# Gated linear attention with a max-out layer behind it: the first three units and the loop's steps put in another order, with dummy matmuls in the gaps

## The chip, the core and the metric

The kernel runs on one core of a Trainium2 chip. A core has five engines with a queue of their own each: TensorE (PE in the profile; its weight loads are PEld), VectorE (DVE), ScalarE (ACT), GpSimd (POOL) and SyncE (SP), which here only issues loads. The metric is the device time of one execution in microseconds (us). It is compared as the median of several executions.

## The reference

Inputs are q, k, v and alpha of shape 4 x 8 x 768 x 48 (batch, head, time, head dimension) and three weight matrices. For every batch and head a 48 x 48 state is carried through time; then all heads of one time step are joined to one row of 384 values, and a two-branch layer is applied.

```python
for t in range(S):
    state = alpha[:, :, t, :, None] * state + np.einsum('bhd,bhe->bhde', k[:, :, t], v[:, :, t])
    y[:, :, t] = np.einsum('bhd,bhde->bhe', q[:, :, t], state)
...
x = np.ascontiguousarray(attn_out.transpose(0, 2, 1, 3)).reshape(B * S, H * D)
g = np.maximum(x @ w1, x @ w2)
return (g @ w_out).astype(np.float32)
```

There are 3072 rows of x, 384 columns, and 1024 hidden columns. The output is 3072 x 384 in float32.

## The kernel before, in words

**Units.** Time is cut into 6 chunks of 128 steps and the batch into 2 groups of 2, which makes 12 units; unit u holds chunk u // 2 of group u % 2. `bb` (0 or 1) is the batch inside a unit. The state passes from unit u to unit u + 2, so units 0 and 1 have no state ahead of them.

**Steps of one unit.** `load` (L85) puts the DMAs of alpha, k, q and v on SP's queue: two for alpha, one each for k, q, v (in units 0 and 1 one for each batch). `ln` (L157) takes the logarithm of alpha on ACT. `sums` (L171) forms running sums of it by matmul (tile `cs`, L181) and per-half totals (L184), and ACT takes exponentials: `Em` (L193), `cs` in place (L195) and `de` (L197). `kmul` (L214, POOL) and `qmul` (L218, DVE) scale k and q; `vcast` (L164, POOL) turns v into 16 bit; `state` (L199, POOL) scales the carried state. `turn` (L222) transposes scaled k and q on PE into one PSUM tile `tp`, which DVE copies to `qk`. `kv` (L232) is K^T V on PE, added into `tm` by DVE. `pairs` (L255) gives the 128 x 128 products `pp` on PE, which DVE multiplies by a triangular mask into `pt` (L265). `ystate` (L267) and `yin` (L281) add up y in PSUM, ACT copies it to `xn`; `xturn` (L296) transposes it on PE and DVE copies it to `xt`. In units 0 and 1 `yfirst` and `xfirst` (L306, L319) do the last three for one batch at a time. `hid` (L341) makes a quarter of the hidden layer: 6 matmuls and a ReLU into `gT`, on ACT for quarters 0 to 2 and on DVE for quarter 3. `hidhalf` (L327) does half the hidden layer for one batch. `outp` (L359) makes 128 rows of output: 3 matmuls of `xt` by `w2o` and 8 of `gT` by `wo16`, a copy on ACT, and with n = 1 the output's DMA, issued from ACT's queue.

**Weights.** max(a, b) is taken as ReLU(a - b) + b. So the hidden layer uses w12 = w1 - w2 (`wsub`, L402, DVE, a quarter at a time), and b W_out is x (w2 w_out): `wturn` (L378) casts a third of w2 on ACT, transposes it on PE and copies it on DVE; `wmul` (L387) multiplies it by w_out in two halves of 12 matmuls, and ACT copies the product to `w2o`. `dummies` (L408) issues matmuls of 512 columns on a zero tile; nothing reads them.

**What sets the order.** The order is written out by hand (L422 to L511), and every engine works its own queue in just that order. PSUM comes from four rings: "g" with 4 buffers (cs, tp, kv, ya, xp), "pp" with 2 (pp), "m" with 2 (hp, op, wt, dummies). A step that takes a buffer waits until its last reader is done. Loads have 4 buffers for each input.

## Time and profile before

| what | value |
|---|---|
| median of 13 runs | 165.71 us (165.07 to 166.66) |
| profiled execution | 165.52 us, its span 163.8 us |
| mean granted PE clock | 0.937 |
| PE busy | 143.8 us, 88% of the span |
| DVE, ACT, POOL busy | 92.6, 79.9, 47.1 us |
| read from and written to memory | 23.59 and 4.72 MB |

The span runs from the first to the last instruction; 1.7 us lie around it. The profile's page cuts the span into 40 slices with a digit for the busy tenths of each engine; the row PEclk gives the clock that PE was granted in tenths. A row of a timeline gives start and length in us, engine, line, operation, tile written and tiles read, how many such instructions follow each other, and in brackets the idle time before it and what ended that. A row of the view by windows gives the stretch, its length, then busy time with the number of instructions for PE, PEld, DVE, ACT and POOL, the granted clock, the share of the 16 DMA engines and GB/s.

### The profile page before, as it was taken

The numbers are of one execution on the slowest core, as the hardware profiler recorded it, in microseconds if no ns is written. First come the engines' busy times: TensorE is split into PE (matmuls) and PEld (weight loads), VectorE is DVE, ScalarE is ACT, GpSimd is POOL, SyncE is SP. The second block draws the span as 40 slices with busy tenths as digits, with TensorE's granted clock in tenths as the row PEclk, the third lists the DMA queues.
The fourth block names the chain that finished last, engine by engine and source line by source line (L and its number), as shares of the span: only waits on it lengthen the run. The fifth ranks groups of instructions, "written<-read, shape, count | busy, mean of one in ns | idle before, by whom it ended". The sixth has DMA issues, their size and how long they took to land.

```text
span 163.8 us, 4099 instructions
## 1 busy us (share of the span) xinstructions
PE 143.8 (88%) x1673; PEld 99.7 (61%) x1673; DVE 92.6 (57%) x191; ACT 79.9 (49%) x166; POOL 47.1 (29%) x73
## 2 busy tenths in 40 slices
PE   6845689994598969999999999999999999999892
PEld 2234435743476557676776776867767677676660
DVE  5064765107604986839569486595774955746110
ACT  3445041861058266737466375563764646643431
POOL 5023220033006280811706208054090350800000
PEclk9996556999569999999999999999999999999999
DMA  4999999999899997995993997989999962020202
GB/s 93 217 365 247 366 313 148 194 189 240 159 200 190 168 240 135 167 195 136 195 205 91 211 257 128 212 183 210 241 186 230 181 92 98 4 96 0 100 0 96
DMA packets 93459, 28.58 MB, mean 174 GB/s; under 512 B 87424, under 2 KB 93056, under 8 KB 93440
## 3 DMA queue, kind: packets, MB, share of 16 engines
q1 hardware_dynamic: 90160, 23.60, 79.4%
q10 hardware_dynamic: 3280, 4.72, 8.7%
q8 instruction: 13, 0.21, 0.6%
q14 instruction: 6, 0.05, 0.1%
HBM read 23.59 MB, written 4.72 MB: 173 GB/s over the span
## 4 chain that ended last, share of the span: by engine, by line
PE 74%; DVE 12%; ACT 5%; DMA 2%; issue 2%; POOL 1%; SPq 0%; ACTq 0%; DVEq 0%
PE op L368 19%; PE hp L350 18%; PE op L366 8%; PE pp L263 4%; PE tp L227 4%; PE wq L395 4%; DVE xt L304 3%; DVE pt L265 3%; PE cs L181 3%; DMA af<-in_alpha_dram 2%; PE ya L287 2%; DVE qk L229 2%; PE xp L302 2%; PE cs L184 2%; PE kv L243 2%
## 5 line engine op out<-in xcount | busy, mean ns | idle before, releaser
L216 POOL TENSOR_TENSOR kn<-kf,Em 128x384 f16<-128x384 f32 x24 | 23.5, 998 | 90.0 <-PE pp L263 48.3
L368 PE MATMUL op<-wo,gT 128*128 128x384 f16 x192 | 35.1, 326 | 0.0
L350 PE MATMUL hp<-xt,w 128*128 128x256 f16 x264 | 32.5, 273 | 2.7 <-DVE xt L304 2.7
L265 DVE TENSOR_TENSOR pt<-pp,u 128x512 f16<-128x512 f32 x48 | 30.9, 684 | 4.0 <-PE pp L263 3.6
L350 PEld LDWEIGHTS <-w 128*128 128x128 f16 x264 | 25.0, 97 | 7.9 <-issue 4.3
L355 ACT ACTIVATE gT<-hp 128x512 f16<-128x512 f32 x33 | 19.7, 597 | 16.7 <-PE hp L350 15.3
L368 PEld LDWEIGHTS <-gT 128*128 128x128 f16 x192 | 18.8, 98 | 12.4
L371 ACT COPY outs<-op 128x384 f32<-128x384 f32 x24 | 11.5, 478 | 28.8 <-PE op L368 28.7
L229 DVE COPY qk<-tp 128x1024 f16<-128x1024 f16 x24 | 16.4, 687 | 6.6 <-PE tp L227 6.5
L220 DVE TENSOR_TENSOR qn<-qf,cs 128x384 f16<-128x384 f32 x24 | 12.3, 549 | 10.8 <-ACT de L197 7.0
L251 DVE TENSOR_TENSOR tm<-kv,sb 64x192 f32<-64x192 f32 x32 | 11.3, 355 | 9.2 <-PE kv L243 8.4
L366 PE MATMUL op<-w2o,xt 128*128 128x384 f16 x72 | 15.8, 329 | 0.3 <-DVE gT L357 0.2
L193 ACT ACTIVATE Em<-cs 128x384 f32<-128x384 f32 x24 | 11.7, 487 | 8.6 <-PE cs L184 8.6
L304 DVE COPY xt<-xp 128x768 f16<-128x768 f16 x10 | 5.6, 557 | 14.5 <-PE xp L302 14.5
L263 PE MATMUL pp<-qk 48*128 48x128 f16 x192 | 11.2, 224 | 2.3 <-DVE qk L229 2.2
L357 DVE TENSOR_SCALAR gT<-hp 128x512 f16<-128x512 f32 x11 | 7.5, 685 | 7.9 <-PE hp L350 7.6
L195 ACT ACTIVATE cs<-cs 128x384 f32<-128x384 f32 x24 | 11.7, 489 | 0.0
L160 ACT ACTIVATE lg<-af 128x768 f16<-128x768 f32 x12 | 10.1, 840 | 3.4 <-DMA af<-in_alpha_dram 3.4
L227 PE MATMUL tp<-ident,qn 128*128 128x128 f16 x96 | 9.8, 227 | 1.7 <-DVE qn L220 1.6
L169 POOL CAST v<-vf 128x768 f16<-128x768 f32 (+1 forms) x14 | 10.2, 732 | 0.8 <-DMA vf<-in_v_dram 0.8
L227 PE MATMUL tp<-ident,kn 128*128 128x128 f16 x96 | 9.5, 222 | 0.8 <-POOL kn L216 0.8
L263 PEld LDWEIGHTS <-qk 48*128 48x128 f16 x192 | 6.2, 96 | 4.9 <-DVE qk L229 2.9
(60 smaller groups left out, 158.6 us busy)
## 6 DMA issues: line engine op xcount, KB each, us to landing
af<-in_alpha_dram SPq DMA_DIRECT2D x24, 192.0 KB, 5.5
out_dram<-outs ACTq DMA_DIRECT2D x11, 384.0 KB, 4.6
kf<-in_k_dram SPq DMA_DIRECT2D x10, 384.0 KB, 6.2
qf<-in_q_dram SPq DMA_DIRECT2D x10, 384.0 KB, 4.6
vf<-in_v_dram SPq DMA_DIRECT2D x10, 384.0 KB, 6.3
w2f<-in_moe_w_dram SPq DMA_DIRECT2D x3, 512.0 KB, 5.1
wof<-in_moe_w_out_dram SPq DMA_DIRECT2D x2, 768.0 KB, 6.9
w1f<-in_moe_w_dram SPq DMA_DIRECT2D x4, 384.0 KB, 8.7
```

Of the source, the lines that this page charges most:

```text
L193: nc.scalar.activation(out=Em, in_=csv[bb], func=ACTF.Exp, scale=-1.0)
L195: nc.scalar.activation(out=csv[bb], in_=csv[bb], func=ACTF.Exp)
L216: nc.gpsimd.tensor_mul(out=X["kn"][bb][:, :, 0:D], in0=X["kf"][:, bb], in1=X["Em"][bb])
L220: nc.vector.tensor_mul(out=X["qn"][bb][:, :, 0:D], in0=X["qf"][:, bb], in1=X["csv"][bb])
L227: nc.tensor.transpose(tp[:, n, j, :], pair(src, j), ident)
L229: nc.vector.tensor_copy(out=qk, in_=tp)
L263: nc.tensor.matmul(pa[a][:, j, :], lhsT=qk[r, 1, j, :], rhs=qk[r, 0, j, :], start=True, stop=True)
L265: nc.vector.tensor_mul(out=pt[:, a], in0=pa[a], in1=u16.unsqueeze(1).to_broadcast([128, HP, C]))
L350: nc.tensor.matmul(hp[:, n, :], lhsT=w12[:, ds, f * 128 : (f + 1) * 128], rhs=X["xt"][:, ds].rearrange("p n t -> p (n t)"), start=(ds == 0 ...
L355: nc.scalar.activation(out=gT[:, 2 * f2 : 2 * f2 + 2, :], in_=hp, func=ACTF.Relu)
L366: nc.tensor.matmul(op, lhsT=X["xt"][:, ds, n, :], rhs=w2o[:, ds, :], start=(ds == 0), stop=False)
L368: nc.tensor.matmul(op, lhsT=X["gT"][:, f, n * C : (n + 1) * C], rhs=wo16[:, f, :], start=False, stop=(f == NF - 1))
```

## The change

Nothing is computed in another way, except that `hidhalf` is gone and unit 1 uses `hid`, like all other units. The rest is order. `sums` is cut so that the exponentials are steps of their own (`expm`, `expp`, `expd`; `exps` is all of them), and the small sums come first. `first` gives way to `scale` (kmul, qmul, vcast), `turn`, `kv` and `pairs` written one by one. The casts of w2 leave `wturn`, those of w_out leave `wmul` (`wcast`), and so do the copies to `w2o` (`wout`). Unit 1's alpha is loaded ahead of w1. In units 0 and 2 there are 39 dummy matmuls in place of 17.

```diff
+    load_alpha(1)
     for n in range(4):
...
         nc.sync.dma_start(out=w1f[:, :, f], in_=moe_w1.rearrange("(s p) f -> p s f", p=128)[:, :, f])
-    load_alpha(1)
...
     dummies(10)
     ln(0)
     sums(0)
-    dummies(4)
-    first(0, 0)
+    exps(0)
+    dummies(6)
+    scale(0, 0)
+    for ds in range(ND):
+        nc.scalar.copy(out=w2h[:, ds, :], in_=w2f[:, ds, :])
+    turn(0, 0)
+    kv(0, (0,))
+    dummies(2)
+    pairs(0, 0)
+    dummies(2)
     wturn(0)
     yfirst(0, 0)
+    dummies(2)
     wturn(1)
+    dummies(2)
     xfirst(0, 0)
     wturn(2)
-    first(0, 1)
+    scale(0, 1)
+    dummies(2)
+    turn(0, 1)
+    kv(0, (1,))
+    dummies(3)
+    pairs(0, 1)
     load(2)
-    dummies(3)
+    dummies(6)
+    wcast(0)
     yfirst(0, 1)
+    wmul(0)
     xfirst(0, 1)
-    wmul(0)
+    wcast(1)
     wmul(1)
-    for n in range(4):
-        wsub(n)
-        hid(0, n)
-
     ln(1)
-    outp(0, 0)
+    wout()
+
     sums(1)
     load(3)
+    wsub(0)
+    wsub(1)
+    hid(0, 0)
+    expm(1, 0)
+    hid(0, 1)
+    expp(1, 0)
+    wsub(2)
+    wsub(3)
+    hid(0, 2)
+    expm(1, 1)
+    expp(1, 1)
+    scale(1, 0)
+    hid(0, 3)
+    expd(1)
+    turn(1, 0)
+    kv(1, (0,))
+    outp(0, 0)
+    scale(1, 1)
+    pairs(1, 0)
+    load(4)
+    turn(1, 1)
+    kv(1, (1,))
+    yfirst(1, 0)
     outp(0, 1)
-    first(1, 0)
-    load(4)
-    yfirst(1, 0)
-    first(1, 1)
+    pairs(1, 1)
+    ln(2)
     xfirst(1, 0)
-    hidhalf(1, 0, 0)
-    hidhalf(1, 0, 1)
+    sums(2)
+    dummies(2)
     yfirst(1, 1)
-    ln(2)
-    outp(1, 0)
-    sums(2)
+    exps(2)
+    dummies(2)
     xfirst(1, 1)
-    hidhalf(1, 1, 0)
-    hidhalf(1, 1, 1)
     for bb in range(2):
         kmul(2, bb)
+    state(2)
+    vcast(2)
+    for bb in range(2):
         qmul(2, bb)
-    vcast(2)
-    state(2)
+    hid(1, 0)
+    hid(1, 1)
+    turn(2, 0)
+    hid(1, 2)
+    turn(2, 1)
+    hid(1, 3)
     load(5)
-    turn(2, 0)
-    turn(2, 1)
...
     for u in range(2, NU):
+        pairs(u, 0)
+        kv(u)
         if nxt:
             ln(u + 1)
-        kv(u)
-        pairs(u, 0)
         if u > 2:
-            hid(u - 1, 2)
-            hid(u - 1, 3)
+            hid(u - 1, 0)
+            hid(u - 1, 1)
         else:
-            outp(1, 1)
+            outp(1, 0)
         if nxt:
             sums(u + 1)
+            exps(u + 1)
...
-        ystate(u)
         pairs(u, 1)
         if u > 2:
-            outp(u - 1, 0)
+            hid(u - 1, 2)
+        ystate(u)
+        if u > 2:
+            hid(u - 1, 3)
...
         yin(u)
+        outp(u - 1, 0 if u > 2 else 1)
         if nxt:
             turn(u + 1, 0)
-        if u > 2:
-            outp(u - 1, 1)
         xturn(u)
         if nxt:
             turn(u + 1, 1)
-        hid(u, 0)
-        hid(u, 1)
+        if u > 2:
+            outp(u - 1, 1)
...
-    hid(NU - 1, 2)
-    hid(NU - 1, 3)
+    for f2 in range(4):
+        hid(NU - 1, f2)
```

Three places in the queues follow; line numbers before and after differ, the tiles' names do not.

ACT in unit 0, before: from the first cast of w2 (w2h) to unit 1's logarithm (lg).

```order
L379 CAST w2h<-w2f 128x1024
L317 CAST xn<-yb 128x384
L379 CAST w2h<-w2f 128x1024 x2
L317 CAST xn<-yb 128x384
L391 CAST wo_168<-wof 128x768 x2
L400 CAST w2o<-wq 128x384 x3
L355 ACTIVATE gT<-hp 128x512 x3
L160 ACTIVATE lg_128<-af 128x16x48
```

ACT in unit 0, now:

```order
L431 CAST w2h<-w2f 128x1024 x3
L333 CAST xn<-yb 128x384
L404 CAST wo_168<-wof 128x768
L333 CAST xn<-yb 128x384
L404 CAST wo_168<-wof 128x768
L160 ACTIVATE lg_128<-af 128x16x48
L401 CAST w2o<-wq 128x384 x3
L357 ACTIVATE gT<-hp 128x512
L197 ACTIVATE Em<-cs 128x384
```

All casts of w2 now stand ahead of the first copy of y (xn), unit 1's logarithm stands ahead of the copies to w2o, and its exponentials stand between unit 0's ReLUs (gT).

ACT in one iteration of the loop, before: ReLUs of two units (gT), the next unit's logarithm and exponentials, the copies of the output (outs) and of y (xn).

```order
L355 ACTIVATE gT<-hp 128x512 x2
L160 ACTIVATE lg_130<-af 128x16x48
L355 ACTIVATE gT<-hp 128x512
L193 ACTIVATE Em<-cs 128x384
L195 ACTIVATE cs<-cs 128x384
L193 ACTIVATE Em<-cs 128x384
L195 ACTIVATE cs<-cs 128x384
L197 ACTIVATE de<-cs 128x16
L371 COPY outs<-op 128x384
L294 CAST xn<-ya 128x8x48 x2
L371 COPY outs<-op 128x384
L376 DMA out_dram<-outs 128x2x384
```

ACT in one iteration of the loop, now:

```order
L160 ACTIVATE lg_130<-af 128x16x48
L357 ACTIVATE gT<-hp 128x512 x2
L197 ACTIVATE Em<-cs 128x384
L202 ACTIVATE cs<-cs 128x384
L197 ACTIVATE Em<-cs 128x384
L202 ACTIVATE cs<-cs 128x384
L207 ACTIVATE de<-cs 128x16
L357 ACTIVATE gT<-hp 128x512
L310 CAST xn<-ya 128x8x48 x2
L373 COPY outs<-op 128x384 x2
L378 DMA out_dram<-outs 128x2x384
```

The logarithm now stands ahead of both ReLUs, and the third ReLU stands behind all exponentials instead of ahead of them.

DVE in one iteration, before: the state's sums (tm), the masked products (pt), the fourth ReLU, scaled q (qn) and three copies out of PSUM.

```order
L251 TENSOR_TENSOR tm<-kv,sb 64x192 x4
L265 TENSOR_TENSOR pt<-pp,u_137 128x512 x2
L357 TENSOR_SCALAR gT<-hp 128x512
L265 TENSOR_TENSOR pt<-pp,u_137 128x512 x2
L220 TENSOR_TENSOR qn_150<-qf,cs 128x8x48
L220 TENSOR_TENSOR qn_154<-qf,cs 128x8x48
L229 COPY qk<-tp 128x1024
L304 COPY xt<-xp 128x768
```

DVE in one iteration, now:

```order
L281 TENSOR_TENSOR pt<-pp,u_137 128x512 x2
L267 TENSOR_TENSOR tm<-kv,sb 64x192 x4
L281 TENSOR_TENSOR pt<-pp,u_137 128x512 x2
L359 TENSOR_SCALAR gT<-hp 128x512
L236 TENSOR_TENSOR qn_150<-qf,cs 128x8x48
L236 TENSOR_TENSOR qn_154<-qf,cs 128x8x48
L245 COPY qk<-tp 128x1024
L320 COPY xt<-xp 128x768
```

The first two masks changed places with the state's sums, and the ReLU went behind the second two masks.

## The prediction, written before the change was timed

> **What bounds the kernel now.** I began with the page, its first two parts.

> ```profile
> PE 143.8 (88%) x1673; PEld 99.7 (61%) x1673; DVE 92.6 (57%) x191; ACT 79.9 (49%) x166; POOL 47.1 (29%) x73
> ...
> PE   6845689994598969999999999999999999999892
> ...
> PEclk9996556999569999999999999999999999999999
> DMA  4999999999899997995993997989999962020202
> ```

> From slice 16 on PE is busy nearly all the time: the loop is bound by PE. Ahead of that, in some 65 us, PE has gaps, and twice its clock falls to half. The DMA engines are busy through the whole of that stage. So the second view is by windows; its columns behind the length are PE, PEld, DVE, ACT, POOL, clock, DMA share, GB/s.

> ```profile
> 10.00:13.40 3.40, 1.73 (x30) 1.10 (x27) 3.19 (x6) 0.89 (x2) 0.00 (x0) 1.00 1.20 296
> 13.40:16.80 3.40, 2.14 (x21) 2.14 (x22) 0.96 (x2) 2.15 (x3) 1.50 (x2) 0.50 1.15 277
> ...
> 20.20:23.60 3.40, 2.60 (x16) 1.13 (x15) 1.77 (x4) 1.60 (x3) 0.83 (x1) 0.50 1.10 345
> 23.60:27.00 3.40, 3.40 (x12) 1.55 (x11) 2.95 (x4) 0.34 (x1) 0.00 (x0) 0.50 1.30 164
> 27.00:30.40 3.40, 3.40 (x25) 2.36 (x24) 0.43 (x1) 1.98 (x4) 0.00 (x0) 0.99 0.99 171
> ...
> 37.30:40.70 3.40, 1.43 (x28) 0.95 (x25) 3.06 (x6) 0.07 (x1) 0.83 (x2) 1.00 1.25 244
> ...
> 44.10:47.50 3.40, 3.15 (x33) 2.98 (x33) 0.19 (x1) 0.99 (x2) 0.00 (x0) 0.50 1.10 193
> ...
> 57.80:61.20 3.40, 2.29 (x38) 1.79 (x38) 3.37 (x7) 2.07 (x6) 3.29 (x5) 1.00 1.03 260
> ```

> The clock changes at 13.4, 27.0, 40.7 and 47.5 us, distances that are multiples of 3.4. It is lost behind a window in which PE was busy 51% (1.73 of 3.40) or 42%, and kept behind one with 67%. It comes back behind windows of 100% and 93%, not behind one of 76%. These bounds serve below.

> Third, PE's timeline, for checkpoints that both kernels pass.

> ```profile
> 14.66 1.04 PE L382 MATMUL wt<-ident,w2h 128*128 128x128 f16 x8 [1.51 <-ACT w2h L379]
> ...
> 23.26 5.91 PE L395 MATMUL wq<-wo,w2T 128*128 128x384 f16 x24 [0.23 <-ACT wo L391]
> 29.01 2.97 PE L350 MATMUL hp<-xt,w 128*128 128x256 f16 x24
> ```

> ```profile
> 42.10 0.60 PE L263 MATMUL pp<-qk 48*128 48x128 f16 x8 [0.47 <-DVE qk L229]
> 44.35 2.72 PE L335 MATMUL hh<-xt,w 128*128 128x128 f16 x24 [1.21 <-DVE xt L325]
> ...
> 60.53 0.39 PE L227 MATMUL tp<-ident,qn 128*128 128x128 f16 x4
> ...
> 72.08 1.47 PE L350 MATMUL hp<-xt,w 128*128 128x256 f16 x12 [0.20 <-DVE xt L304]
> 76.50 0.56 PE L263 MATMUL pp<-qk 48*128 48x128 f16 x8
> ```

> Unit 0's hidden layer ends at 31.98, unit 1's second pairs at 42.70, unit 3's second turn at 60.92.

> **A. Unit 0, to the end of its hidden layer.** Now wt waits 1.51 us for a cast of w2 that stands behind the copy of y on ACT; moved ahead, three casts of 1.05 us are done when wt wants them, and the copy of y is some 0.2 us later. Twenty-two dummies are added in all, 18 of them here, at 0.215 us each (512 columns, from 1.30 us for 8 of 384 in the last row of E). They fill waits; five of them fall in the window from 10.0 to 13.4, which goes to 1.73 + 1.1 = 2.8 us busy, 83%, so the clock stays. Then the 24 matmuls of wq take 3.9 us, not 5.91, and end at 24.6 in place of 29.2. This is not all gained, since w1 is not there yet.

> ```profile
> 26.48 0.96 DVE L404 TENSOR_TENSOR w<-w1f,w2f 128x768 f16<-128x768 f32 x1 [0.45 <-DMA w1f<-in_moe_w_dram]
> ```

> ```profile
> 13.47 3.09 SPq L102 DMA_DIRECT2D w1f<-in_moe_w_dram  x4
> 16.61 4.18 SPq L68 DMA_DIRECT2D af<-in_alpha_dram  x2
> ...
> 22.28 3.52 SPq L80 DMA_DIRECT2D qf<-in_q_dram  x1
> ...
> 29.31 0.71 SPq L80 DMA_DIRECT2D vf<-in_v_dram  x1
> ```

> The last quarter of w1 landed at 26.4. With 393 KB of alpha put ahead of it, it lands between 26.4 (if they share bandwidth anyway, as before) and 28.8 (2.4 us at 164 GB/s); I take 28.0. Subtraction 0.96, last quarter of hid 0.65: the end is 29.65, **2.3 us** earlier. The 3.9 us of dummies cost nothing as long as PE waits here for w1; without that cover they would cost up to 2.9, the time by which PE is early. They also delay nothing on SP, whose loads wait for no PE step here.

> **B. Unit 1, to the end of its second pairs.** Its loads pace it.

> ```profile
> qf<-in_q_dram SPq DMA_DIRECT2D x1, 192.0 KB, 7.4
> ```

> ```profile
> vf<-in_v_dram SPq DMA_DIRECT2D x1, 192.0 KB, 4.6
> ```

> These are the transfers issued at 22.28 and 29.31: q of the first batch lands at 29.7, v of the second at 33.9. SP's queue issues without a pause, and the bytes ahead of them are the same, so I leave them there. Chain: qn 0.55, turn to 30.6; v's cast and kv to 31.4; outp(0,0) 1.8, 33.2; pairs and turn 34.05; cast of the last v 0.5, kv to 34.8; yfirst 0.45, outp 1.8, pairs 0.4: 37.6. Before, this piece took 10.72 us, now 7.95: **2.8 us** less. The added wait: ACT's `de` of unit 1 now stands behind DVE's qn (it comes later in the program); behind it wait the copies of outp, which PE needs only at 33.2, so it costs nothing unless q lands 2 us later.

> The clock takes back some. In the window 27.0 to 30.4 PE has two hid quarters (1.30) and a turn (0.35): 1.65 us, 49%, like the two windows that lost it. From 30.4 to 33.8 it is 79% busy, nearest to the 76% that did not bring it back; so half speed until about 37.2. Work of some 3 us on the path doubles, of which 0.7 hides in the wait for v: **+2.3 us**; the ends are 0 (no loss) and 3.

> [...]

> **C. From there to the end of unit 3's second turn**: 18.22 us before, of them 1.21 us waiting in the row at 44.35 and half speed to 47.5. Now: copy of outp and issue of the output's DMA 0.9, ln(2) 0.84, sums 0.7 (39.75); dummies 0.43, yfirst 0.45, copy 0.48, first Em 0.49 and kn 1.0 with hid beside them; turns and hid to 45.3; pairs and kv 0.75, outp 1.8, sums 0.7, pairs 0.35 (48.9); masks of these 1.3 and yin (50.5); outp 1.8, two turns and xturn 1.25: 53.55. That is 15.95, **2.3 us** less. The two dummies behind sums are on this path (0.43); the other two wait beside ACT's copy. hid in place of hidhalf is worth 0.1 at full clock: half the matmuls, the same columns.

> **D. The loop.**

> ```profile
> 72.08:135.02 62.94, 61.73 (x817) 45.30 (x816) 43.64 (x85) 36.03 (x78) 22.35 (x30) 1.00 1.01 184
> ```

> Six iterations of 10.49. Of these 0.37 is PE's wait for xt (the row at 72.08 shows 0.20 to the modelled end of the matmuls before): now outp, pairs and kv stand between xturn and hid, 2.5 us against 0.56 for DVE's copy. 0.16 is the second pairs waiting for the masks (0.56 against 0.40 for the first); masks now go ahead of tm, and pairs has 2.7 us. What is late next: hid's third ReLU stands behind the exponentials on ACT.

> ```profile
> L265 DVE TENSOR_TENSOR pt<-pp,u 128x512 f16<-128x512 f32 x48 | 30.9, 684 | 4.0 <-PE pp L263 3.6
> L355 ACT ACTIVATE gT<-hp 128x512 f16<-128x512 f32 x33 | 19.7, 597 | 16.7 <-PE hp L350 15.3
> ```

> Counted from the first pairs: sums ends at 2.73, five exponentials 1.75, ReLU 0.6: 5.1. The first outp, which needs that PSUM buffer, could start at 5.0, so 0.17 is lost. Second masks: pairs ends at 3.06, two of 0.68 end at 4.4, yin starts at 4.6. Period 10.49 - 0.37 - 0.16 + 0.17 = 10.13; I take 10.15 (bounds 9.9, no ReLU stall and other short waits gone, and 10.49, all given back). Seven iterations, 73.9 before (60.92 to 134.82), 71.05 now: **2.85 us** less.

> **E. The end.**

> ```profile
> 153.20 0.57 DVE xt L304
> ...
> 153.81 1.47 PE hp L350 x12
> ...
> 157.46 1.30 PE op L368 x8
> ```

> 134.82 to 163.8 is 28.98 before. Now 9.8 for unit 10, 7.85 for unit 11 up to its last outp (pairs 0.66, four hid 2.62, ystate and yin 0.63, two outp 3.58, xturn 0.33), then hid 2.97, outp 3.78 and the tail 3.24, unchanged: 27.6, **1.4 us** less, most of it waits for xt as in this row.

> Sum: -2.3 - 2.8 + 2.3 - 2.3 - 2.85 - 1.4 = -9.35. The profiled execution took 165.52 us, so 156.2; the median lies 0.2 above it. **156.3 us.**

> **Rivals.** R1: the clock holds everywhere. For it, a window of unit 1 may straddle the gap with about 60% busy, since windows need not start where they do in this trace. Then 156.3 - 2.3 = 154.0.

> R2: loads come late.

> ```profile
> HBM read 23.59 MB, written 4.72 MB: 173 GB/s over the span
> ```

> ```profile
> 30.00:60.00 30.00, 24.30 (x288) 16.74 (x286) 14.76 (x29) 14.90 (x33) 8.71 (x12) 0.89 1.17 199
> ```

> Without 4.72 MB of weights a unit reads 1.57 and writes 0.39 MB. At the saturated 199 GB/s that is 9.9 us, under 10.15. But the lead of the loads shrinks.

> ```profile
> 45.38 2.14 SPq L80 DMA_DIRECT2D vf<-in_v_dram  x1
> ```

> ```profile
> vf<-in_v_dram SPq DMA_DIRECT2D x1, 384.0 KB, 7.2
> ```

> This is v of unit 3: it lands at 52.6 and its cast ends at 53.4. kv used it at 62.6 before and wants it near 56.2 now; 9 us of lead become 3. A loss of 5% of bandwidth up to there takes that, and with about 0.55 us for each of six units behind it the time is 159.5.

> R3: the dummies do not hold the clock in units 0 and 2. Unit 0 cold costs 1.2 (wq ends at 27.5, the rest hides behind w1), unit 2 cold from 40.7 to 44.1 costs 1.7: 159.2. My windows there are 77% and 63% busy, the second within the unknown stretch.

> [...]

> ```profile
> 57.80:61.20 3.40, 1.24 (x16) 1.02 (x16) 1.00 1.03 260
> ```

> ```profile
> 57.80:61.20 3.40, 0.51 (x6) 0.34 (x6) 1.00 1.03 260
> ```

> These are the transposes of turn and xturn: 1.75 of the 2.29 us of a window behind which the clock stayed.

> R4, slower: supply as the bound from unit 1 to the end. If denser use drops it to 171 GB/s, a unit needs 11.5 us; v of unit 11 lands at 33.9 + 115 = 148.9, behind it come cast 0.8 and 14.3 of PE work: span 164.0, 165.7 us. From 11.5 us on the change loses; at 11.8, 168.7. For it: single slices at 153 to 180 GB/s. Against it: v of units 1 and 3 landed 18.7 us apart (33.9 and 52.6), 9.35 for each.

> **Numbers.** Forecast 0.46, R1 0.20, R2 0.16, R3 0.12, R4 0.04, and 0.02 that gains and losses meet within 0.3%, about what a measurement of this kernel tells from no change. Range 152.6 to 160.8: from R1 with a period of 9.95, to the forecast with all of D given back and a late load or unit 2 cold. Faster 0.94, same 0.02, slower 0.04.

> **What would show it.** A: no clock below 1.0 before 27 us, wq in 3.9 us, and DVE's subtractions waiting for w1. B: kv of unit 1 waiting for v at 34, clock 0.5 for one or two windows from about 30. C: unit 3's second turn near 56 with that loss. D: a period of 10.1 to 10.2, no wait for xt, a short wait of outp for ACT. It would be wrong if ACT's logarithm waits for alpha in the loop (R2), if a period of 10.5 shows that the ReLU's wait is larger, or if the clock row has more than one dip.

## The result, and the profile after

The changed kernel takes 155.19 us (median of 11 runs, 154.24 to 156.35) where the kernel before took 166.02 beside it: a ratio of 0.9353, 95% interval 0.9329 to 0.9377. Forecast were 156.3 us and a range of 152.6 to 160.8. The profiled execution took 155.38 us, its span 153.6, 10.2 less than before. Two executions further down lie more than 1.5% above the fastest of their kernel (158.03 us with late outputs, 157.54 with the log early); as for the kernel before, such executions count in the medians and not in the ratios. The page of the changed kernel, parts 1 and 2:

```profile
PE 140.2 (91%) x1671; PEld 95.9 (62%) x1671; DVE 93.2 (61%) x192; ACT 78.5 (51%) x165; POOL 47.5 (31%) x73
...
PE   6778898787799989899999999999999999999991
...
PEclk9999999999999999999999999999999999999999
DMA  3999999999999799997999999999999992020202
```

In this execution the clock row has no dip left; the forecast had one. By windows (columns as before: length, then PE, PEld, DVE, ACT, POOL, clock, DMA share, GB/s):

```profile
10.00:13.40 3.40, 2.82 (x37) 1.60 (x35) 3.17 (x6) 2.58 (x3) 0.00 (x0) 1.00 1.12 295
...
27.00:30.40 3.40, 2.55 (x22) 1.45 (x20) 2.29 (x4) 2.84 (x7) 1.00 (x2) 1.00 0.96 166
37.20:40.60 3.40, 2.03 (x29) 1.04 (x27) 1.55 (x3) 1.23 (x3) 0.00 (x0) 1.00 0.97 214
75.00:125.00 50.00, 50.00 (x680) 37.17 (x674) 36.36 (x70) 29.11 (x65) 18.66 (x25) 1.00 1.22 212
53.52:64.76 11.24, 10.39 (x136) 7.47 (x137) 8.27 (x16) 5.36 (x12) 3.77 (x5) 1.00 1.15 202
```

The loop from 75 to 125 us has no wait on PE at all. Its one bad piece is the last row, the iteration of unit 3, which is 1.2 us longer than the 10.06 of those behind it. PE's timeline at the checkpoints:

```profile
22.27 2.11 PE L394 MATMUL wq<-wo,w2T 128*128 128x384 f16 x12 [0.22 <-ACT wo L404]
...
28.91 0.83 PE L352 MATMUL hp<-xt,w 128*128 128x256 f16 x6 [0.42 <-DVE w L409]
...
36.85 0.40 PE L279 MATMUL pp<-qk 48*128 48x128 f16 x8
...
38.89 0.35 PE L180 MATMUL cs<-halves,lg 128*128 128x4 f16 x8 [1.37 <-ACT lg L160]
...
41.77 1.47 PE L352 MATMUL hp<-xt,w 128*128 128x256 f16 x12 [0.45 <-DVE xt L341]
...
53.52 0.40 PE L279 MATMUL pp<-qk 48*128 48x128 f16 x8
...
56.08 0.35 PE L180 MATMUL cs<-halves,lg 128*128 128x4 f16 x8 [0.41 <-ACT lg L160]
...
61.87 0.40 PE L243 MATMUL tp<-ident,qn 128*128 128x128 f16 x4 [0.44 <-DVE qn L236]
...
64.76 0.40 PE L279 MATMUL pp<-qk 48*128 48x128 f16 x8
```

Unit 0's hidden layer ends at 29.74 (before 31.98), unit 1's second pairs at 37.25 (42.70), unit 3's second turn at 53.52 (60.92). Between 53.52 and 64.76 stand two waits, for a logarithm and for the scaled q. DVE's and ACT's timelines tell what those two waited for:

```profile
27.89 0.96 DVE L409 TENSOR_TENSOR w<-w1f,w2f 128x768 f16<-128x768 f32 x1 [0.29 <-DMA w1f<-in_moe_w_dram]
29.67 0.55 DVE L236 TENSOR_TENSOR qn<-qf,cs 128x384 f16<-128x384 f32 x1 [0.81 <-DMA qf<-in_q_dram]
...
61.25 1.02 DVE L236 TENSOR_TENSOR qn<-qf,cs 128x384 f16<-128x384 f32 x2 [1.61 <-DMA qf<-in_q_dram]
```

```profile
55.18 0.84 ACT L160 ACTIVATE lg<-af 128x768 f16<-128x768 f32 x1 [2.38 <-DMA af<-in_alpha_dram]
```

Unit 4's alpha and q came late; so did w1 and unit 1's q further ahead, as forecast.

### The profile page after: what moved, and what is told of

It is laid out like the page before. It is cut to its first block, busy times and chain, and to the rows that moved or that the text cites. A ratio compares the mean times of both kernels' runs of the same rounds, so it can differ in the third digit from the quotient of the medians.

```text
span 153.6 us, 4086 instructions
## 1 busy us (share of the span) xinstructions
PE 140.2 (91%) x1671; PEld 95.9 (62%) x1671; DVE 93.2 (61%) x192; ACT 78.5 (51%) x165; POOL 47.5 (31%) x73
## 3 DMA queue, kind: packets, MB, share of 16 engines
q1 hardware_dynamic: 90160, 23.60, 87.3%
q10 hardware_dynamic: 3280, 4.72, 8.8%
HBM read 23.59 MB, written 4.72 MB: 184 GB/s over the span
## 4 chain that ended last, share of the span: by engine, by line
PE 66%; SPq 15%; DMA 9%; ACT 3%; DVE 2%; issue 1%; ACTq 1%; POOL 0%; DVEq 0%
PE op L370 19%; PE hp L352 17%; PE op L368 8%; SPq L80 8%; DMA qf<-in_q_dram 6%; PE tp L243 5%; SPq L103 4%; DMA vf<-in_v_dram 4%; PE pp L279 3%; PE cs L186 3%; PE kv L259 2%; PE ya L303 2%; PE xp L318 2%; SPq L68 2%; DVE pt L281 2%; PE ya L291 2%
## 5 line engine op out<-in xcount | busy, mean ns | idle before, releaser
L352 PE MATMUL hp<-xt,w 128*128 128x256 f16 x288 | 37.6, 273 | 1.9 <-DVE w L409 1.2
L281 DVE TENSOR_TENSOR pt<-pp,u 128x512 f16<-128x512 f32 x48 | 30.9, 686 | 13.1 <-PE pp L279 12.6
L373 ACT COPY outs<-op 128x384 f32<-128x384 f32 x24 | 11.5, 479 | 42.3 <-PE op L370 42.3
L352 PEld LDWEIGHTS <-w 128*128 128x128 f16 x288 | 25.7, 98 | 7.6 <-DVE w L409 2.4
L357 ACT ACTIVATE gT<-hp 128x512 f16<-128x512 f32 x36 | 20.4, 594 | 3.7 <-PE hp L352 3.4
L160 ACT ACTIVATE lg<-af 128x768 f16<-128x768 f32 x12 | 10.1, 843 | 12.4 <-DMA af<-in_alpha_dram 8.3
L368 PE MATMUL op<-w2o,xt 128*128 128x384 f16 x72 | 15.6, 325 | 0.0
L359 DVE TENSOR_SCALAR gT<-hp 128x512 f16<-128x512 f32 x12 | 8.3, 691 | 8.7 <-PE hp L352 8.7
L416 PE MATMUL warm<-wz 128*128 128x512 f16 x39 | 12.4, 445 | 1.3 <-DVE halves L123 1.3
L169 POOL CAST v<-vf 128x768 f16<-128x768 f32 (+1 forms) x14 | 10.2, 731 | 5.8 <-DMA vf<-in_v_dram 5.8
L202 ACT ACTIVATE cs<-cs 128x384 f32<-128x384 f32 x24 | 11.8, 491 | 0.0
L243 PE MATMUL tp<-ident,qn 128*128 128x128 f16 x96 | 9.3, 219 | 1.4 <-DVE qn L236 1.4
L279 PE MATMUL pp<-qk 48*128 48x128 f16 x192 | 9.5, 217 | 0.2 <-DVE qk L245 0.2
## 6 DMA issues: line engine op xcount, KB each, us to landing
af<-in_alpha_dram SPq DMA_DIRECT2D x24, 192.0 KB, 5.3
out_dram<-outs ACTq DMA_DIRECT2D x11, 384.0 KB, 4.4
kf<-in_k_dram SPq DMA_DIRECT2D x10, 384.0 KB, 6.0
qf<-in_q_dram SPq DMA_DIRECT2D x10, 384.0 KB, 7.7
vf<-in_v_dram SPq DMA_DIRECT2D x10, 384.0 KB, 7.7
w1f<-in_moe_w_dram SPq DMA_DIRECT2D x4, 384.0 KB, 8.4
```

Source lines behind the costliest of these rows:

```text
L243: nc.tensor.transpose(tp[:, n, j, :], pair(src, j), ident)
L279: nc.tensor.matmul(pa[a][:, j, :], lhsT=qk[r, 1, j, :], rhs=qk[r, 0, j, :], start=True, stop=True)
L281: nc.vector.tensor_mul(out=pt[:, a], in0=pa[a], in1=u16.unsqueeze(1).to_broadcast([128, HP, C]))
L352: nc.tensor.matmul(hp[:, n, :], lhsT=w12[:, ds, f * 128 : (f + 1) * 128], rhs=X["xt"][:, ds].rearrange("p n t -> p (n t)"), start=(ds == 0 ...
L357: nc.scalar.activation(out=gT[:, 2 * f2 : 2 * f2 + 2, :], in_=hp, func=ACTF.Relu)
L368: nc.tensor.matmul(op, lhsT=X["xt"][:, ds, n, :], rhs=w2o[:, ds, :], start=(ds == 0), stop=False)
```

## The experiments

Each group of four runs shared a chip and the runs of the kernel before there. Three ideas were to be tested: in the front the loads set the pace, and a clock loss hurts only where no load covers it; the clock goes by the busy share of windows of 3.41 us (in the trace of before its changes, at 13.40, 27.05, 40.71 and 47.53 us, lie multiples of that apart); the loop won because the wait for xt and the waits for masks went. The rivals stand with each run. The table gives starts of PE steps in the profiled executions (pairs(u,n) is the step `pairs`), the iteration of unit 3 (pairs(3,0) to pairs(4,0)), and the period from there on.

| kernel | us, median | ratio to before, 95% | pairs(1,1) | pairs(3,0) | iteration 3 | period | span |
|---|---|---|---|---|---|---|---|
| changed | 155.19 | 0.9353 (0.9329 to 0.9377) | 36.85 | 53.52 | 11.24 | 10.06 | 153.6 |
| 17 dummies | 154.57 | 0.9312 (0.921 to 0.9414) | 37.13 | 53.37 | 10.48 | 10.06 | 152.8 |
| transposes | 156.60 | 0.9416 (0.9315 to 0.9517) | 38.69 | 55.37 | 11.16 | 10.07 | 155.5 |
| no unit 2 dummies | 155.75 | 0.934 (0.924 to 0.944) | 37.22 | 56.33 | 10.05 | 10.06 | 155.3 |
| late outputs | 155.95 | 0.936 (0.9264 to 0.9457) | 37.19 | 53.41 | 10.04 | two of 11.02, 10.58 | 153.9 |
| new front, old loop | 160.10 | 0.9629 (0.9561 to 0.9697) | 37.41 | 59.17 | 10.76 | 10.50 | 159.8 |
| old front, new loop | 165.17 | 0.9923 (0.9882 to 0.9963) | 41.89 | 62.68 | 10.17 | 10.17 | 162.4 |
| alpha behind w1 | 160.22 | 0.9631 (0.957 to 0.9692) | 41.80 | 59.57 | 10.04 | 10.06 | 158.6 |
| no w1 | 152.37 | 0.9198 (0.9129 to 0.9268) | 34.72 | 51.39 | 10.05 | 10.06 | 150.6 |
| K^T V first | 159.20 | 0.9577 (0.954 to 0.9614) | 37.07 | 54.43 | 11.17 | 10.53 | 156.9 |
| outputs at the end | 154.69 | 0.9289 (0.9257 to 0.932) | 37.81 | 53.82 | 10.05 | 10.07 | 153.1 |
| the same, log early | 155.43 | 0.9339 (0.93 to 0.9379) | 38.79 | 54.02 | 10.04 | 10.09 | 153.4 |
| changed, again | 155.91 | 0.9369 (0.9333 to 0.9404) | 37.94 | 54.60 | 10.39 | 10.07 | 153.9 |

Some of these profiled executions ran windows at half clock: one in the runs with late outputs and with the log early, two without unit 2's dummies and with the new front and the old loop, three with 17 dummies and with alpha behind w1, seven with the old front (the kernel before: six). Their starts hold that loss.

### Do the dummies earn anything?

```diff
     exps(0)
-    dummies(6)
+    dummies(4)
...
     kv(0, (0,))
-    dummies(2)
     pairs(0, 0)
-    dummies(2)
...
-    dummies(6)
+    dummies(3)
     wcast(0)
```

> The changed kernel's order, with the dummies of the kernel before alone: 10, 4 and 3 in place of 39. Theory 1 (the granted clock goes by PE's busy share in a window of some 3.4 us; it is lost behind windows of about half and less): the window from 10.0 to 13.4 falls from 83% to some 45% busy, the clock is lost at 13.4 as in the kernel before and comes back between 23.6 and 27. Unit 0's part of that is partly hidden behind the loads of w1 (0 to 1.4 us); the window from 37.2 falls to 47%, which would cost another 0.9 to 2.6. Time 156 to 159. [...]

All 22 added dummies are out, those of unit 2 too. 154.57 us: not slower than the changed kernel, and by the intervals not told apart from it. Windows on the grid on which the clock changed in that execution:

```profile
8.63:12.04 3.41, 1.92 (x28) 1.32 (x28) 2.38 (x5) 2.30 (x4) 0.71 (x2) 1.00 1.04 375
12.04:15.45 3.41, 2.81 (x29) 2.47 (x30) 2.32 (x5) 1.67 (x3) 0.99 (x1) 0.50 1.22 198
...
18.87:22.28 3.41, 3.41 (x17) 1.45 (x16) 1.19 (x2) 1.77 (x3) 1.31 (x2) 0.50 1.21 241
22.28:25.69 3.41, 3.41 (x32) 2.21 (x32) 1.32 (x2) 1.91 (x4) 0.00 (x0) 1.00 1.09 341
```

The theory of the busy share fits here: the clock was lost behind a window with PE 56% busy (1.92 of 3.41), and the first half of `wq` took 3.03 us instead of 2.11. Yet unit 0's hidden layer ends at 29.91 against 29.74: the three slow windows hide behind the load of w1. In unit 0 the dummies bought a clock that this stage did not need. Of the 0 to 1.4 us that I gave for it, 0.17 came. In unit 2 the clock stayed in this execution, behind windows of 60 and 70%; another of the four took 156.61 us with a mean clock of 0.956 instead of 0.964. Nor did the dummies hold the clock in every run: the one with late outputs has the changed kernel's unit 0, and it ran from 7.86 to 11.27 us at half clock, behind a window 47% busy.

### Is a transpose busy for the clock?

```diff
     def dummies(n):
-        warm = new("m", [128, 512], FP32, 2, "warm")
-        for _ in range(n):
-            nc.tensor.matmul(warm, lhsT=wz[:, 0:128], rhs=wz, start=True, stop=True)
+        warm = new("m", [128, 8, 128], FP16, 2, "wart")
+        for i in range(4 * n):
+            nc.tensor.transpose(warm[:, i % 8, :], wz[:, 128 * (i % 4) : 128 * (i % 4) + 128], ident)
```

> All dummies but the first ten are replaced by four transposes each, of 128 columns of the same zeros: the same columns through PE, another kind of instruction. If transposes count as busy for the clock (what the trace of before showed in one window, 1.75 of 2.29 busy us): clock 1.00 throughout, 155.2 within 0.5. [...]

The mean clock was 1.00 in three executions and 0.997 in the fourth. One window of the profiled execution, on the grid of its clock record, which starts at 5.50 us and shows no loss up to 155.69: PE as a whole first, then all in it that is not a transpose, the matmuls into yb (PE, clock, DMA share, GB/s).

```profile
12.33:15.74 3.41, 2.85 (x52) 2.68 (x53) 2.29 (x5) 1.78 (x3) 1.00 (x1) 1.00 1.05 186
```

```profile
12.33:15.74 3.41, 0.35 (x7) 1.00 1.05 186
```

PE is 84% busy with the transposes and 10% without, and the clock stayed at 1.00. (The records overlap at their ends: from 13.40 to 16.80 us of this run the transposes into wart, wt, tp and xb stand with 3.39 us in sum, and PE as a whole with 2.63. So what is left beside transposes is read from its own rows and not as a difference; that holds for the 1.75 of 2.29 us in the prediction too.) The median of 156.6 is not told apart from 155.2 by its interval; in the profiled execution the second quarter of `hid` waited 1.52 us for w1, which moved everything behind it. Why w1 came late there is open.

### What do the four dummies of unit 2 hold?

```diff
     sums(2)
-    dummies(2)
     yfirst(1, 1)
     exps(2)
-    dummies(2)
     xfirst(1, 1)
```

> Only the four dummies of unit 2 (two behind the sums, two behind the exponentials) are taken out. They are 0.87 us of the 2.03 that PE is busy in the window from 37.2 to 40.6. Theory 1 (busy share): without them that window is 35 to 47% busy, the clock is lost near 40.6 and comes back one or two windows later; 0.43 comes off the path, 0.9 to 2.6 is added: 156 to 157.5. [...]

Median 155.75, but the four executions differ: 154.98 us with a mean clock of 1.00, 155.51 and 155.99 with 0.989, 157.01 with 0.978. One window of 3.41 us at half clock is 0.011 of such a span, so the same program lost none, one or two. The profiled one lost two:

```profile
37.29:40.70 3.41, 1.69 (x31) 0.96 (x31) 1.55 (x3) 1.64 (x3) 0.00 (x0) 1.00 0.99 208
40.70:44.11 3.41, 2.75 (x14) 1.92 (x15) 1.38 (x3) 2.42 (x7) 2.70 (x4) 0.50 1.25 260
```

50% busy, and lost, with 1.36 us as the longest wait in the window; in the kernel before the window that lost it at 13.40 us had none longer than 0.62. With the clock kept (one execution, 154.98 us) the 0.43 us that the dummies take cannot be told from the spread. With it lost, unit 3 begins 2.81 us later (56.33 against 53.52), of which iteration 3 gives 1.19 back, because unit 4's loads are no longer late. Where the grid of windows falls would explain that one program loses none, one or two: counted back to the start of the span, it begins at 1.8 us in the run with 17 dummies, at 3.2 here, and at 0.8 in the run with alpha behind w1. It is not shown, as only one of the four executions left a trace.

### Which load is late, and why?

```diff
-        elif n == 1:
+        elif n == 1 and u > 1:
             nc.scalar.dma_start(out=dst, in_=X["outs"])
...
+        if u in (5, 6):
+            late(u - 5)
```

`late` is the output's DMA, issued by ACT; `outs` has four buffers.

> The outputs of units 0 and 1 (0.39 MB each) are written to memory in iterations 5 and 6 of the loop, from buffers of their own, so that 0.79 MB less moves ahead of unit 4's loads. Iteration 3 took 11.24 us against 10.06 of the others, because alpha, q and v of unit 4 come late. If they are late because the loads share bandwidth that is used up (198 GB/s of reads and writes from 30 to 60 us): they land up to 4 us earlier, iteration 3 falls to 10.1 to 10.4, time 154.2. If the order or the waits of the queue hold them, or writes cost the reads nothing: no change, 155.2.

The logarithm of unit 4's alpha starts at 54.28 in place of 55.18, and iteration 3 falls from 11.24 to 10.04, as it should if loads and outputs share bandwidth. Two executions of the changed kernel differ here, 11.24 and 10.39, but the table bears it out: 10.04 or 10.05 in all three runs with these outputs late, 10.39 to 11.24 in the four with them early, w1 loaded, the same loop and pairs(3,0) before 55.4. But the time stays: the iterations of units 6 and 7 take 11.02 and 10.58. ACT's timeline of this run shows that bandwidth is not what holds unit 6:

```profile
84.23 0.38 ACTq L378 DMA_DIRECT2D out_dram<-outs  x1
84.66 0.92 ACTq L383 DMA_DIRECT2D out_dram<-outs  x1
85.67 0.84 ACT L160 ACTIVATE lg<-af 128x768 f16<-128x768 f32 x1 [1.47 <-issue]
```

Two DMA issues in a row on ACT's queue held the logarithm behind them by 1.47 us, and PE's sums waited 0.80 for it. In unit 7 it was 1.03 us and 0.36. I had put a second issue in front of the one ACT step that has no room.

### Front and loop apart

New front, old loop (the loop as before, `outp(1, 0)` ahead of it):

> The changed kernel's front (units 0 to 2) with the loop's order of before. If the loop's own gain is a period of 10.06 in place of 10.49, the loop loses 0.43 in each of some seven iterations and about 1 at the end, less the 1.2 us of unit 4's late loads, which a slower loop partly covers: 158.0 to 159.5, and PE again waits for xt ahead of hid (0.2 to 0.4). If instead the later loop gains only because of where it starts, the time stays within 1 us of 155.2.

160.10, ratio 0.9629, 0.6 over the expectation; the executions with a clock of 1.00 took 159.65 and 159.72. The period is 10.50 again, with both old waits in each iteration, for xt and for masks. PE's timeline of this run:

```profile
62.02 0.38 PE L279 MATMUL pp<-qk 48*128 48x128 f16 x7 [0.18 <-DVE pt L281]
...
68.19 1.47 PE L352 MATMUL hp<-xt,w 128*128 128x256 f16 x12 [0.20 <-DVE xt L320]
```

Old front, new loop (`hidhalf` and the old `sums` stay with the front; it has all of unit 1's work ahead of the loop, and `outp(1, 0)` too):

> The front of before with the changed loop. If the two parts add: 166.0 less 4 to 4.8, so 161.2 to 162.0, with a period of 10.06 and the clock lost at 13.4 and 40.7 as before. Since the loop starts later here, unit 4's loads are not late, and iteration 3 takes 10.1, not 11.2. If the loads set the pace of the later part whatever the front does, more is left: the loop ends as early as in the changed kernel, below 158.

165.17, ratio 0.9923: 1.1 us, not 4 to 4.8. From unit 3's second turn to the end it does gain, 99.7 us (162.4 - 62.68) against 102.9 (163.8 - 60.92). But it reaches that point 1.8 us later, and all of this is lost in unit 2's iteration. PE's timeline there:

```profile
55.99 0.18 PE L275 MATMUL ya<-sb,qk 48*128 48x48 f16 x1 [0.34 <-DVE tm L251]
56.66 0.37 PE L275 MATMUL ya<-sb,qk 48*128 48x48 f16 x15 [0.49 <-DVE tm L251]
...
57.98 0.34 PE L287 MATMUL ya<-v,pt 128*128 128x48 f16 x4 [0.31 <-DVE pt L265]
58.14 1.13 PE L366 MATMUL op<-w2o,xt 128*128 128x384 f16 x3
59.07 2.38 PE L368 MATMUL op<-wo,gT 128*128 128x384 f16 x8
```

With no `outp` between pairs and ystate PE meets DVE's tm and masks (1.14 us of waits), the clock is lost at 57.51, behind a window with PE 72% busy (2.46 of 3.41 us), and outp takes 3.15 instead of 1.78. So the parts do not add: 6.1 and 1.1 apart, 10.3 to 10.8 together. The new loop thus seems to need a front that leaves it outp(1, 0) as cover, as the change's front does; the old front with that one step left over was not run.

### The one load that was moved

```diff
-    load_alpha(1)
     for n in range(4):
         f = slice(n * DFF // 4, (n + 1) * DFF // 4)
         nc.sync.dma_start(out=w1f[:, :, f], ...)
+    load_alpha(1)
```

> The changed kernel, with unit 1's alpha loaded behind w1 as before (0.39 MB moved back). If the bytes ahead set when a load lands: w1's last quarter lands some 2 us earlier (near 25.9), alpha near 28 in place of 19 to 20, so the sums of unit 1 wait for the logarithm until 29, and hid behind them starts late by 2 to 3: 157 to 158. If PE fills that wait, because hid only waited for w1: within 0.3 of 155.2.

160.22: 5 us slower (4.6 by the ratios), about twice what I gave it. PE's timeline:

```profile
29.77 0.38 PE L180 MATMUL cs<-halves,lg 128*128 128x4 f16 x8 [5.32 <-ACT lg L160]
...
30.83 4.78 PE L352 MATMUL hp<-xt,w 128*128 128x256 f16 x24
```

The wait is there, and hid, ready long before, stands behind it in PE's order. What I had left out: behind the window from 24.70 to 28.11, without a single matmul, the clock was 0.50 until 34.94, so hid takes 4.78 where it took 2.97 before.

> w1 is not loaded: the difference is made from two quarters of w2, so the output is not the reference's; the same instructions run on the same tiles' sizes. 1.57 MB less is read ahead of unit 1's loads, so that each later load can land up to 7.9 us earlier. If the loads bind the front in unit 0 (w1), unit 1 (q and v) and unit 4: 1.9 off unit 0, 0.6 off unit 1, 1.2 off iteration 3, so 151 to 152, and the subtractions wait for w2 or nothing. If only w1 binds: 153.3. If PE's own chain binds all along and waits only move: 155.

The edit, for the run without w1: `w12` is made from other quarters of w2, and the four DMAs of w1 are gone, so its output is another one. 152.37. Unit 0's hidden layer ends 1.3 us earlier (28.43), unit 1's second pairs 2.1, and iteration 3 takes 10.05: the span is 3.0 shorter. The loads bind at all three places; in unit 0 less than I gave (1.9), because PE then waits 0.71 us for the cast of w_out. Behind unit 4 nothing more is won, for there PE is the bound.

### What in the loop's order counts?

```diff
     for u in range(2, NU):
         nxt = u + 1 < NU
-        pairs(u, 0)
         kv(u)
+        pairs(u, 0)
```

> In the loop, each unit's K^T V goes ahead of its first pairs again, so that DVE writes tm ahead of the masks; all else as in the changed kernel. If that order is worth what the prediction gave it (0.16 us of waiting for masks in each iteration, more where the shorter loop leaves less room): period 10.15 to 10.25, time 156.3 to 157. If the loop's gain is the wait for xt alone: period 10.06, within 0.3 of the changed kernel on the same chip.

159.20; the period is 10.53, as long as the old loop's, though the wait for xt stays away. PE's and DVE's timelines in one iteration:

```profile
76.12 0.40 PE L279 MATMUL pp<-qk 48*128 48x128 f16 x8
...
78.40 0.22 PE L279 MATMUL pp<-qk 48*128 48x128 f16 x1
78.96 0.38 PE L279 MATMUL pp<-qk 48*128 48x128 f16 x7 [0.35 <-DVE pt L281]
```

```profile
76.13 1.46 DVE L267 TENSOR_TENSOR tm<-kv,sb 64x192 f32<-64x192 f32 x4 [1.05 <-PE kv L259]
77.62 1.29 DVE L281 TENSOR_TENSOR pt<-pp,u 128x512 f16<-128x512 f32 x2
```

The second pairs come 2.28 us behind the first and need their PSUM buffers; DVE reads these until 78.91, because 1.46 us of tm stand ahead. I had priced this at 0.16 from the wait of the kernel before; it is 0.47 in each iteration, of which the row shows 0.35. In the old loop 2.68 us lay between the two pairs (73.82 to 76.50), so the same DVE work showed less. So the masks ahead of tm are needed: without them the wait for xt goes and the period stays as long as before. Whether they would do alone, with hid where it was, was not run.

### A faster version

```diff
+            tag, n2 = ("outs0", 3) if u < 3 else ("outs", 2)
...
-        elif n == 1:
+        elif n == 1 and u > 2:
             nc.scalar.dma_start(out=dst, in_=X["outs"])
...
+        if u in (8, 9, 10):
+            late(u - 8)
```

Here `late` issues from SP's queue, where the last load stands ahead of it.

> The outputs of units 0 to 2 (1.18 MB) are written behind the last load, in iterations 8 to 10, from buffers of their own and by SP's queue; with that ACT issues none of them, so the logarithm of unit 2 can start some 0.45 us earlier. Theory 1 (the loads up to unit 4 and further share a supply that is used up, and late outputs only moved the wait from iteration 3 to iterations 5 and 6, because they were written there): now nothing is written while loads are short, iteration 3 takes 10.1 and none behind it is longer: 153.4 to 154.0 where the changed kernel takes 155.2. Theory 2 (iterations 5 and 6 wait because PE runs ahead of the loads whatever is written): the wait of 1.2 turns up in a later iteration again: 154.8 to 155.2.

> The changed kernel itself, on the chip of these three runs, so that differences below 1 us can be read: 155.2 within 0.6.

154.69 against 155.91 on the same chip, and the intervals of the two ratios do not meet: the outputs of units 0 to 2 behind the last load, issued by SP, gain some 1.2 us. PE's timeline of it, and then of the changed kernel beside it:

```profile
39.19 0.35 PE L180 MATMUL cs<-halves,lg 128*128 128x4 f16 x8 [0.71 <-ACT lg L160]
...
45.68 0.40 PE L279 MATMUL pp<-qk 48*128 48x128 f16 x8
...
53.82 0.40 PE L279 MATMUL pp<-qk 48*128 48x128 f16 x8
...
63.87 0.40 PE L279 MATMUL pp<-qk 48*128 48x128 f16 x8
```

```profile
39.98 0.35 PE L180 MATMUL cs<-halves,lg 128*128 128x4 f16 x8 [1.37 <-ACT lg L160]
...
46.46 0.40 PE L279 MATMUL pp<-qk 48*128 48x128 f16 x8
```

Iteration 3 takes 10.05 and no later one more than 10.4, though PE reaches it 0.78 us earlier than in the changed kernel beside it; the sums of unit 2 wait 0.71 us in place of 1.37, since no issue stands between the copy and the logarithm on ACT. Two things changed at once here. Without the issue ACT's queue brings PE to pairs(2,0) 0.65 us earlier (7.87 us behind pairs(1,1) against 8.52). And unit 4's alpha lands earlier: its logarithm, which waits for it in both, starts at 54.27 against 55.67, so that iteration 3 does not take the gain back (10.05 against 10.39). What each would be worth alone was not run. Theory 1 holds in its gain, 1.2 of the 1.2 to 1.8 that it gave, and in that no long wait turns up later; the time as written, 153.4 to 154.0, was missed, as the changed kernel took 155.91 on this chip and not 155.2.

> As the run with the outputs of units 0 to 2 at the end, and the logarithm of unit 2 ahead of the copy of the second output product on ACT, so that the sums of unit 2 do not wait 1.37 us for it. If its alpha (issued at 29.9 to 31.7, some 6.3 us to landing) is there at 37: 0.4 to 0.9 less than that run, 152.6 to 153.4. If alpha lands later, or the exponentials behind the sums wait for the masks' copy anyway: no difference.

The wait for unit 2's logarithm is gone, and from pairs(1,1) to pairs(3,0) it takes 15.23 us against 16.01. Yet the median is 155.43, not less (the intervals overlap). In the profiled execution the gain went to a clock loss, at 31.37:

```profile
27.96:31.37 3.41, 1.95 (x20) 1.17 (x19) 2.17 (x4) 1.61 (x5) 1.50 (x2) 1.00 1.15 185
31.37:34.78 3.41, 3.41 (x15) 1.47 (x12) 1.34 (x4) 0.00 (x0) 1.50 (x2) 0.50 1.19 199
```

The other executions had a clock of 0.997 and above and took 154.63 to 157.54; what held them is open.

## Why the prediction was right, and where it was not

The time lies 1.1 us under the forecast and 1.2 over R1, in which the clock holds everywhere. In mechanism it was R1 with a part of R2. That the forecast came so close is luck: 2.3 us for a clock loss that did not come stood against 1.8 us that C, D and E fell short.

| term | predicted | measured |
|---|---|---|
| A, unit 0 | -2.3 | -2.24 |
| B, unit 1 to its second pairs | -2.8 | -3.21 |
| clock lost behind 30.4 | +2.3 | 0 |
| C, to unit 3's second turn | -2.3 | -1.95 |
| D, seven iterations | -2.85 | -2.30 |
| E, the end | -1.4 | -0.50 |
| sum | -9.35 | -10.2 |

**A** held by its own steps: 83% busy in the window from 10.0, wq in two pieces of 2.11, the last quarter of w1 at 27.9 (I took 28.0), the end at 29.74 (29.65). That the dummies cost nothing is shown by the run without them. That they serve nothing there, I had not said: I gave their lack 1.2 us (R3), and it was 0.17. Alpha ahead of w1 stood in the sum as a cost on w1; as a gain it is 5 us, the largest of any single edit tried.

**B** held too: q of unit 1 released qn at 29.67 (29.7 predicted), the last v's cast began at 33.57 (33.9). It gained 0.4 more than the sum.

**The clock** was the step that failed. "In the window 27.0 to 30.4 PE has two hid quarters (1.30) and a turn (0.35): 1.65 us, 49%": the row shows 2.55 us, 75% (76% from 26.83 to 30.25, the nearest window on the grid of the changed kernel's own clock record). The quarters do not run back to back but one at a time as w1 arrives, and a quarter alone stands in the records with 0.83 us (two back to back with 1.47), not with its pitch of 0.65; nearly two and a half of them fall into the window, 2.03 us, and the turn with 0.52. I had read the bounds from records and set a pitch against them. The loss itself was no fancy: in the run with the log early it came at 31.37, behind a window with 57%, and outp(0, 0) then took 3.56 us instead of 1.88. So it is a risk of single executions, with a price of up to some 1.7: of the 18 executions of the changed kernel on record two, 156.35 and 156.62 us, have a mean clock of 0.989 and 0.987, which is one window, and the others 0.996 or more. By that my 0.20 for R1 was far too low.

**C** is 0.32 short; the copy, the DMA's issue and the logarithm of unit 2 came as listed (sums at 38.89). The 0.45 us that PE waits for xt at 41.77 had no term in the sum; that this is the 0.32 was not tested.

**D.** The steady period is 10.06 (10.15 predicted), as no wait for xt is left and the third ReLU never stalls outp. But its split was wrong: 0.37 for xt plus 0.16 for masks is not what happens, since with the masks behind tm the period is back at 10.53. And 1.18 was lost once, in iteration 3: R2's mechanism, late alpha and q, but for unit 4 alone. I had named the lead of unit 3's v as the risk; ACT's logarithm waiting for alpha in the loop was my sign for R2, and it came once. The supply then recovers. SP's timeline of the changed kernel, alpha of units 4 and 11:

```profile
47.46 4.14 SPq L68 DMA_DIRECT2D af<-in_alpha_dram  x2
...
114.24 2.29 SPq L68 DMA_DIRECT2D af<-in_alpha_dram  x2
```

Seven units in 66.78 us are 9.54 each, under the period of 10.06. R4, which needed 11.5, is excluded by the same number and by the period itself. The bound on the front shows in the two profiled executions of the changed kernel: the second reached pairs(3,0) 1.08 us later than the first, and pairs(4,0) only 0.23 later. What the front wins beyond 54 us the loads take back.

**E** is 0.9 short: I gave units 10 and 11 0.27 us each less than a full period without a row for it, and the last hidden layer 2.97, in which it now waits 0.29 us for its own ReLU.

## What to carry to other kernels

In these runs a clock loss and the dummies against it had next to no price where something else was late: three windows at half clock in unit 0 of the run with 17 dummies moved the end of its hidden layer by 0.17 us, behind the load of w1. So find first what the stage waits for (here the loads), and write what can wait, such as early outputs, behind the last load and from a queue that has room (worth some 1.2 us here). Waits that stand one behind another on the same step did not add: with K^T V first the wait for xt was gone and the period 10.53, as long as before. So price an order by what the next slowest engine still has to do at that point, not by the wait that the old order showed. And compare busy shares only in the measure in which the bound was read.

## What the runs showed of the hardware

| run | 1.00, lost behind | 1.00, kept behind | 0.50, back to 1.00 behind | 0.50, not back behind |
|---|---|---|---|---|
| before | 51, 42 | 66, 68 | 100, 93 | 63, 62, 77, 57 |
| changed | | 60 | | |
| 17 dummies | 56 | 61, 60, 70, 74 | 100 | 82, 62 |
| transposes | | 48 | | |
| no unit 2 dummies | 50 | 72 | 100 | 81 |
| late outputs | 47 | 72 | 100 | |
| new front, old loop | 60, 66 | | 87, 94 | |
| old front, new loop | 51, 42, 72 | 66 | 100, 92, 91 | 60, 62, 77, 59 |
| alpha behind w1 | 0, 58 | 58 | 100, 87 | 52 |
| the log early | 57 | 74 | | |

The window with 48%, in the run with transposes as dummies, lies on the grid of that run's clock record:

```profile
25.98:29.39 3.41, 1.64 (x12) 1.01 (x12) 1.85 (x3) 1.18 (x3) 0.00 (x0) 1.00 0.95 200
```

From half clock it came back in these traces behind 87% and more, and not behind 82% and less. Between 48 and 72% windows went both ways, so the forecast's loss behind 49% would not have been certain even with its 49%. The two that lost it at 66 and 72% held mostly matmuls of 48 or 64 rows or 48 columns; the one that kept it at 48% held two quarters of `hid`, and one that kept it at 60% mostly outp, both with full rows:

```profile
35.93:39.35 3.42, 2.05 (x26) 1.14 (x25) 1.64 (x4) 1.32 (x2) 0.00 (x0) 1.00 1.34 210
```

(the run with 17 dummies). What told these windows apart was not tested; the one that lost it at 56% in that same run held mostly transposes with full rows.

A DMA's issue on ACT took 0.35 to 0.43 us of its queue in the kernels before and after, and 0.48 in the run with alpha behind w1. A second one right behind it took 0.92 us once and 0.48 once (the run with late outputs); the first of these is more than a logarithm (0.84).
